# Spectral mixing and GEGLU on one core: modulation rows, half of the soft thresholds, and the order of weight preparation, moved between engines

## The chip, the core and the metric

The kernel runs on one core of a Trainium2 chip. A core has TensorE (PE; its weight loads are listed as PEld), VectorE (DVE), ScalarE (ACT), GpSimd (POOL) and SyncE (SP, which here issues every DMA). Each engine works through its own instructions in order and waits on semaphores for the others. SBUF is the on-chip memory, PSUM the accumulators that TensorE writes, 128 partitions each. The metric is the device time of one execution in microseconds (us).

## The reference

Input `x` is 8192 rows of D = 448. A vector `c` gives six modulation rows of 448 (shift, scale and gate for each of two blocks). The first block is a Fourier filter: layer norm, real FFT along the 8192 rows, a complex two-layer MLP in four blocks of 112 channels with a ReLU between, a soft threshold with 0.01, the inverse FFT. The second is a GEGLU with 1792 hidden channels.

```
mod = (_silu(c) @ w_mod).reshape(c.shape[0], 6, 1, -1)
sa, ca, ga, sb, cb, gb = (mod[:, 0], mod[:, 1], mod[:, 2], mod[:, 3], mod[:, 4], mod[:, 5])
h = _layernorm(x, axis=-1) * (1 + ca) + sa
x = x + ga * _A_ref(h, A_w1, A_b1, A_w2, A_b2)
h = _layernorm(x, axis=-1) * (1 + cb) + sb
x = x + gb * _B_ref(h, B_w_gate, B_w_up, B_w_down)
...
lam = 0.01
mr = jnp.abs(or_) - lam
or_ = jnp.sign(or_) * mr * (mr > 0)
```

The threshold equals `y - min(max(y, -lam), lam)`, and also `min(y + lam, relu(y - lam))`.

## The kernel before

The FFT over 8192 = 128 x 64 is done in two stages of matmuls, and every matmul of the filter is split in a high and a low part to keep fp32 accuracy. There are three phases. **Phase A** (to about 80 us) loads `x`, normalises it and does the 128-point transform, storing the result `td` in HBM. **Phase B** (about 80 to 440 us) does the 64-point transform, the filter's MLP, the threshold and the first inverse transform, and beside it prepares what phase C needs. **Phase C** (about 440 us to the end) does the last inverse transform and the GEGLU over 32 chunks of rows, whose down product is a seven-product Strassen form.

Phase B works on 32 units (half of the channels, four frequency rows: `h, bt`) in a software pipeline of steps, `step(i)`. Step i issues the load `tr` of unit i+2; the 64-point transform of unit i on TensorE (`stage_s2`: 24 short matmuls; ACT writes the high part `zh`, then DVE the low part `zl`); the split `th`/`tl` of unit i+1 (ACT, POOL); the second MLP layer, the threshold and the split `yh`/`yl` of unit i-2 in two halves p = 0, 1 (`stage_m2`: DVE writes the clipped value `t` at line 462 and four pieces of `y` at line 470, ACT copies to `yh`, POOL subtracts to `yl`); the inverse transform of unit i-3 (`stage_i1`, ACT copies `us`, which is stored to HBM); and the first MLP layer of unit i-1 (`stage_m1`: ACT writes `hh` with a ReLU, DVE the low part `hl`). The order within a step is written out by hand (`manual_schedule`), and each engine keeps it. A step is counted below from the start of its `zl` on DVE: step 2 begins at 94.27 us, step 12 at 241.25, step 31 at 415.34.

Preparation is hung into the steps through `at(step, hook, function)`, with the hooks `load`, `pe`, `act`, `dve`, `pool` at fixed places of a step: `load` and `pe` stand first, `act` after the split of unit i+1, `dve` after the second half's `yh`, just ahead of `stage_m1`. Hung in are: the four modulation rows `cb`, `sb`, `ga`, `gb` (load of a 448 x 448 matrix as four slices of 112 partitions; `mod_sum` multiplies slice k by `cs[:, k]` and adds, all on POOL, lines 633 to 636; `mod_row` sums over partitions with a ones matmul `psm`, line 640, and ACT copies the row out), `row_scales` (maxima of two rows, as small operations let out one at a time by `drip()`), the norms of the gate and up weights (`squares` on ACT, `norms` on PE, `norms_out` `nrm` on DVE, steps 1 to 16), the seven Strassen combinations of the down weights (`down_sums`: a reduction on DVE, four POOL subtractions on `m`), from step 18 the scaled gate and up weights (`weights_hi` on ACT, `weights_lo` on DVE for pr = 0 and on POOL for pr = 1), and three scaled down weights (`down_hi` on ACT line 867, `down_lo` on DVE line 871).

## Time and profile before

| | |
|---|---|
| median of 3 runs | 2016.21 us (2015.73 to 2016.96) |
| profiled execution | 2015.64 us, span 2013.8 us, mean granted clock 0.977 |
| busy | PE 1914.2 us (95%), DVE 1136.5 (56%), ACT 764.7 (38%), POOL 1232.5 (61%) |
| DMA | 165.75 MB, mean 82 GB/s |

The span is the time from the first to the last instruction; the profiled execution's own time is 1.84 us longer. A row of the timeline gives the start and the length in us, engine, line, operation, what is written and read, its shape and, in square brackets, how long the engine sat idle before it and what ended that. `x2` or `x4` is the number of instructions merged in a row. In the table by windows come, for each stretch, its length, the busy time and number of instructions of PE, PEld, DVE, ACT and POOL, the granted clock of TensorE (1.00 is full speed), the share of DMA busy and GB/s. "Granted clock" is what the throttle let TensorE have.

### The profile page before, as it was taken

What the parts mean: (1) busy time and instruction counts of PE and PEld (TensorE: products, weight loads), DVE (VectorE), ACT (ScalarE), POOL (GpSimd) and SP (SyncE); (2) the same over time, 40 slices, a digit from 0 to 9 for tenths busy, and PEclk for the clock granted to TensorE, in tenths of its full rate; (3) what the DMA queues carried; (4) which work ended last, traced back from release to release, by engine and by line L of the source; (5) the groups of instructions that cost most, each with busy time, mean ns of one, the idle gap of its engine ahead of it and who ended that gap; (6) DMA issues with size and microseconds to landing.
All of it is one profiled execution on the core that took longest, in us unless ns stands there. A gap on an engine that the chain in (4) does not pass through costs nothing.

```text
span 2013.8 us, 43386 instructions
## 1 busy us (share of the span) xinstructions
PE 1914.2 (95%) x17622; PEld 1700.3 (84%) x17622; DVE 1136.5 (56%) x2351; ACT 764.7 (38%) x1286; POOL 1232.5 (61%) x1532
## 2 busy tenths in 40 slices
PE   7857799979999999999999999999999999999999
PEld 3557789967888989898888888888888888889898
DVE  8536689876655555555455555555555555555533
ACT  5534457745233333333333333333333333333322
POOL 4257656636566666666666666666666666666644
PEclk9878899989999999999999999999999999999999
DMA  9856666742211111111111111111111111111000
GB/s 345 296 153 214 218 205 192 215 118 82 62 44 43 43 42 43 43 43 43 43 43 49 44 45 50 42 42 42 46 47 42 42 42 42 43 42 43 22 17 20
DMA packets 147851, 165.75 MB, mean 82 GB/s; under 512 B 83953, under 2 KB 121585, under 8 KB 147266
## 3 DMA queue, kind: packets, MB, share of 16 engines
q1 hardware_dynamic: 147650, 162.97, 26.6%
q8 instruction: 138, 2.26, 0.5%
q14 instruction: 63, 0.52, 0.1%
HBM read 97.49 MB, written 49.66 MB: 73 GB/s over the span
## 4 chain that ended last, share of the span: by engine, by line
PE 82%; DVE 7%; POOL 4%; DMA 2%; ACT 2%; issue 1%; SPq 0%; DVEq 0%; ACTq 0%; POOLq 0%
PE pgu L1034 50%; PE pdn L1102 7%; PE pdn L1100 7%; PE pdn L1101 7%; DVE y L470 2%; PE ps L212 1%; DMA td<-xt 1%; POOL raw L635 1%; PE pi L934 1%; DVE t L462 1%; DVE zl L385 1%; POOL raw L636 1%; PE pi L932 1%; DVE hl L440 1%; PE pi L933 1%
## 5 line engine op out<-in xcount | busy, mean ns | idle before, releaser
L1034 PE MATMUL pgu<-nt,wh 128*128 128x256 f16 x6272 | 834.3, 273 | 1.6 <-DVE nt L1025 1.6
L1034 PEld LDWEIGHTS <-wh 128*128 128x128 f16 x6272 | 602.7, 98 | 99.3 <-issue 31.7
L1070 ACT ACTIVATE gel<-pgu,dg 128x256 f32<-128x256 f32 x448 | 200.3, 473 | 797.4 <-PE pgu L1034 762.1
L1034 PE MATMUL pgu<-nt,wl 128*128 128x256 f16 (+1 forms) x3584 | 501.3, 272 | 0.0
L1100 PE MATMUL pdn<-wd,ac 128*128 128x224 f16 x1568 | 406.1, 259 | 2.0 <-ACT p L1129 2.0
L1102 PE MATMUL pdn<-wd,ac 128*128 128x224 f16 x1568 | 406.1, 259 | 0.2 <-DVE ac L1093 0.2
L1101 PE MATMUL pdn<-wd,ac 128*128 128x224 f16 x1568 | 406.1, 259 | 0.0
L1081 POOL TENSOR_TENSOR x<-x 128x128 f32<-128x128 f32 x223 | 243.4, 1091 | 235.5 <-DVE x L1075 235.5
L1093 DVE SCALAR_TENSOR_TENSOR ac<-x,sa_act,ac 128x896 f16<-128x896 f32 (+1 forms) x225 | 310.4, 1380 | 84.6 <-ACT ac L1092 84.6
L1034 PEld LDWEIGHTS <-wl 128*128 128x128 f16 (+1 forms) x3584 | 297.9, 97 | 57.2 <-issue 23.9
L1075 DVE TENSOR_TENSOR x<-pgu,gel 128x256 f32<-128x256 f32 x448 | 179.6, 418 | 285.0 <-ACT gel L1070 284.4
L1092 ACT ACTIVATE ac<-x,sa_act 128x896 f16<-128x896 f32 (+1 forms) x225 | 232.9, 1035 | 52.5 <-POOL x L1084 50.5
L1135 POOL TENSOR_TENSOR o<-u,p 128x224 f32<-128x224 f32 x32 | 21.1, 658 | 291.9 <-DVE u L1134 291.9
L1082 POOL TENSOR_TENSOR x<-x 128x128 f32<-128x128 f32 x223 | 159.1, 714 | 17.5
L1101 PEld LDWEIGHTS <-ac 128*128 128x128 f16 x1568 | 153.4, 98 | 2.5 <-issue 2.2
L1100 PEld LDWEIGHTS <-ac 128*128 128x128 f16 x1568 | 153.4, 98 | 0.6 <-issue 0.2
L1102 PEld LDWEIGHTS <-ac 128*128 128x128 f16 x1568 | 153.4, 98 | 0.5 <-DVE ac L1093 0.5
L108 POOL TENSOR_TENSOR yl<-y,yh 128x448 fp32r<-128x448 f32 x63 | 77.7, 1234 | 76.6 <-ACT yh L106 75.4
L1083 POOL TENSOR_TENSOR x<-x 128x128 f32<-128x128 f32 x223 | 114.7, 514 | 0.0
L1084 POOL TENSOR_TENSOR x<-x 128x128 f32<-128x128 f32 x223 | 107.6, 483 | 0.0
L470 DVE TENSOR_TENSOR y<-pm,t 64x224 f32<-64x224 f32 x256 | 99.5, 389 | 8.6 <-DVE t L462 0.5
L108 POOL TENSOR_TENSOR tl<-tr,th 128x896 f16<-128x896 f32 x30 | 57.3, 1910 | 71.3 <-ACT th L106 59.3
(291 smaller groups left out, 2824.7 us busy)
## 6 DMA issues: line engine op xcount, KB each, us to landing
tr<-td SPq DMA_DIRECT2D x64, 224.0 KB, 4.6
raw<-in_gu SPq DMA_DIRECT2D x28, 512.0 KB, 6.3
vd<-us SPq DMA_DIRECT2D x64, 224.0 KB, 3.0
xx<-in_x SPq DMA_DIRECT2D x32, 448.0 KB, 3.3
v<-vd SPq DMA_DIRECT2D x64, 224.0 KB, 2.8
out<-x SPq DMA_DIRECT2D x31, 448.0 KB, 2.7
nt<-pk SPq DMA_TRANSPOSE x480, 2.3
tb<-in_x SPq DMA_DIRECT2D x8, 896.0 KB, 17.5
```

The lines of the kernel that those rows point to most:

```text
L108: (el or V).tensor_tensor(lo, src, h, ALU.subtract)
L470: V.tensor_tensor(y[ri * 64 : ri * 64 + 64, gi], pv[si, ri], tv[si, ri], ALU.subtract)
L1034: T.matmul(pgu[i, t, q][:, pr * H : (pr + 1) * H], w[rows, tw, f0 : f0 + 128], nts[i][rows, tn, :], start=start, stop=stop, skip_group_che ...
L1070: S.activation(gl, ps[:, :H], AF.Gelu_apprx_tanh, scale=dg)
L1075: V.tensor_tensor(dst, ps[:, H : 2 * H].rearrange("p (b c) -> p b c", b=2), gl.rearrange("p (b c) -> p b c", b=2), ALU.mult)
L1081: e.tensor_tensor(s1, a21, a22, ALU.add)
L1082: e.tensor_tensor(s2, s1, a11, ALU.subtract)
L1092: S.activation(ac[:, 0, k], x[:, k], AF.Copy, scale=sc)
L1093: V.scalar_tensor_tensor(ac[:, 1, k], x[:, k], sc, ac[:, 0, k], op0=ALU.mult, op1=ALU.subtract)
L1100: T.matmul(ps, ac[:, 0, ka], wds[t][:, 0, kb], start=t == 0, stop=False)
L1101: T.matmul(ps, ac[:, 0, ka], wds[t][:, 1, kb], start=False, stop=False)
L1102: T.matmul(ps, ac[:, 1, ka], wds[t][:, 0, kb], start=False, stop=t == NP - 1)
```

## The change

Four things change, all in phase B.

1. **Modulation rows.** The matrix is loaded whole into one tile `wm` (one buffer) in place of two DMAs into the shared `raw` buffers. `mod_sum` multiplies the four slices on ACT (`Copy` with a per-partition scale) and adds two pairs in one POOL instruction of 896 columns; the last addition, `mod_sum2`, comes one step later in the `act` hook; and the ones matmul follows one step after that. Loads move from the `load` hook of steps 1, 3, 5, 8 to the `dve` hook of steps 1, 4, 7, 10; the products to steps 2, 5, 8, 11, `mod_sum2` to 3, 6, 9, 12 and the ones matmul to 4, 7, 10, 13 (from 3, 5, 7, 10).
2. **Soft threshold.** The half p = 1 of each unit is formed as `min(y + lam, relu(y - lam))`: the ReLU by ACT, with the bias in a tile `neglam`, in place of DVE's clip, and the four pieces of `y` by a `scalar_tensor_tensor` on DVE in place of a subtraction.
3. **Down combinations** are loaded in steps 2, 3, 5, 6, 9, 11, 12 (from 4, 6, 7, 9, 11, 12, 14) and formed a step later; `row_scales` moves from step 6 to 7.
4. **Scaled down weights** are made in steps 23, 25, 27 (from 23, 26, 29).

```diff
+    neglam = cpool.tile([128, 1], F32, name="neglam")
+    V.memset(neglam, -LAM)
...
-            V.tensor_scalar(t, ps[:, :D], LAM, -LAM, op0=ALU.min, op1=ALU.max)
+            if p:
+                S.activation(t, ps[:, :D], AF.Relu, bias=neglam)
+            else:
+                V.tensor_scalar(t, ps[:, :D], LAM, -LAM, op0=ALU.min, op1=ALU.max)
...
-                    V.tensor_tensor(y[ri * 64 : ri * 64 + 64, gi], pv[si, ri], tv[si, ri], ALU.subtract)
+                    o = y[ri * 64 : ri * 64 + 64, gi]
+                    if p:
+                        V.scalar_tensor_tensor(o, pv[si, ri], LAM, tv[si, ri], op0=ALU.add, op1=ALU.min)
+                    else:
+                        V.tensor_tensor(o, pv[si, ri], tv[si, ri], ALU.subtract)
...
-            return pool.tile([128, 4, 256], F32, tag="raw", name="raw", bufs=6 if pool is npool else 4)
+            return pool.tile([128, 4, 256], F32, tag="raw", name="raw", bufs=4)
...
-            out = []
-            for i in range(2):
-                wm = raw_tile(pool).rearrange("p q c -> p (q c)")[:112, : 2 * D].rearrange("p (q c) -> p q c", q=2)
-                dma(wm, wmod[q][:, 2 * i : 2 * i + 2])
-                out += [wm[:, 0], wm[:, 1]]
-            return out
+            wm = pool.tile([112, 4, D], F32, tag="wm", name="wm", bufs=1)
+            dma(wm, wmod[q])
+            return wm
 
         def mod_sum(key):
             r = raws[key]
-            G.tensor_scalar(r[0], r[0], cs[:, 0:1], None, op0=ALU.mult)
-            for k in range(1, 4):
-                G.tensor_scalar(r[k], r[k], cs[:, k : k + 1], None, op0=ALU.mult)
-                G.tensor_tensor(r[0], r[0], r[k], ALU.add)
+            for k in range(4):
+                S.activation(r[:, k], r[:, k], AF.Copy, scale=cs[:, k : k + 1])
+            G.tensor_tensor(r[:, 0:2], r[:, 0:2], r[:, 2:4], ALU.add)
+
+        def mod_sum2(key):
+            r = raws[key]
+            G.tensor_tensor(r[:, 0], r[:, 0], r[:, 1], ALU.add)
...
-        for n, (key, q, dst) in zip((1, 3, 5, 8), (("cb", 4, cb_r), ("sb", 3, sb_r), ("ga", 2, ga_r), ("gb", 5, gb_r))):
-            at(n, "load", pre, npool, key, load_mod_row, q)
+        for n, (key, q, dst) in zip((1, 4, 7, 10), (("cb", 4, cb_r), ("sb", 3, sb_r), ("ga", 2, ga_r), ("gb", 5, gb_r))):
+            at(n, "dve", pre, npool, key, load_mod_row, q)
             at(n + 1, "dve", mod_sum, key)
-            at(n + 2, "pe", mod_row, key, dst)
+            at(n + 2, "act", mod_sum2, key)
+            at(n + 3, "pe", mod_row, key, dst)
...
-        for t, n in enumerate((4, 6, 7, 9, 11, 12, 14)):
+        for t, n in enumerate((2, 3, 5, 6, 9, 11, 12)):
...
-        at(6, "dve", row_scales)
+        at(7, "dve", row_scales)
...
-            at(22 + 3 * t, "load", load_d, fp, t, 1)
-            at(23 + 3 * t, "act", down_hi, t)
-            at(23 + 3 * t, "dve", down_lo, t)
+            at(22 + 2 * t, "load", load_d, fp, t, 1)
+            at(23 + 2 * t, "act", down_hi, t)
+            at(23 + 2 * t, "dve", down_lo, t)
```

Three places where the order of an engine moves. First POOL, from step 6 on, before: the second half's `yl`, the seven operations of a modulation row, and the first two of `row_scales` (line 515 is the helper that lets them out).

```order
L108 TENSOR_TENSOR yl<-y,yh 128x448 x2
L633 TENSOR_SCALAR raw<-raw,cs 112x448
L635 TENSOR_SCALAR raw<-raw,cs 112x448
L636 TENSOR_TENSOR raw<-raw 112x448
L635 TENSOR_SCALAR raw<-raw,cs 112x448
L636 TENSOR_TENSOR raw<-raw 112x448
L635 TENSOR_SCALAR raw<-raw,cs 112x448
L636 TENSOR_TENSOR raw<-raw 112x448
L515 TENSOR_SCALAR cb_r<-cb_r 128x448
L515 TENSOR_SCALAR hb<-rmax 128x1
L108 TENSOR_TENSOR tl<-tr,th 128x896
```

In the change the row's work on POOL is two additions in two steps, with the next unit's `tl` between them (here the second row, steps 5 to 7):

```order
L641 TENSOR_TENSOR wm<-wm 112x896
L110 TENSOR_TENSOR tl<-tr,th 128x896
L645 TENSOR_TENSOR wm<-wm 112x448
L110 TENSOR_TENSOR yl<-y,yh 128x448 x2
L795 TENSOR_TENSOR m<-m 128x224
L796 TENSOR_TENSOR m<-m 128x224
L797 TENSOR_TENSOR m<-m 128x224
L798 TENSOR_TENSOR m<-m 128x224
L110 TENSOR_TENSOR tl<-tr,th 128x896
L110 TENSOR_TENSOR yl<-y,yh 128x448 x2
```

The pair addition (line 641) follows step 5's `yl`, and the last addition (line 645) stands before step 6's; the seven operations in a row are gone. The next five rows are again four down combinations, those of step 7, and then `cb_r`, the first of `row_scales`. Then ACT in step 5 (in the change the step of a modulation row's products), from the first half's `yh` to `zh` of the next step:

```order
L108 CAST yh<-y 128x448
L465 ACTIVATE t<-pm_1442,neglam 128x448
L511 COPY us<-pi_1463 128x448
L511 COPY us<-pi_1468 128x448
L108 CAST yh<-y 128x448
L640 ACTIVATE wm<-wm,cs 112x448 x4
L441 ACTIVATE hh_759<-pm_1484 112x2x256
L441 ACTIVATE hh_760<-pm_1500 112x2x256
L386 ACTIVATE zh_755<-ps_1536,ca_101 112x2x256
```

The `t` of the second half (line 465) stands behind the first half's `yh`, and the four products (line 640) stand ahead of both `hh`; before, `yh`, `us`, `us`, `yh`, `hh`, `hh` followed each other. Last DVE in step 7, where the rows' maxima are taken (`t`, `y` of the first half, `y` of the second, `hl`):

```order
L467 TENSOR_SCALAR t<-pm_1731 128x448
L479 TENSOR_TENSOR y<-pm_1731,t 64x224 x4
L477 SCALAR_TENSOR_TENSOR y<-pm_1755,t 64x224 x4
L791 TENSOR_REDUCE dn<-m 128x1
L442 SCALAR_TENSOR_TENSOR hl<-pm_1800,hh_759 112x2x256
L442 SCALAR_TENSOR_TENSOR hl<-pm_1817,hh_760 112x2x256
L524 TENSOR_REDUCE rmax<-cb_r 128x1
L688 TENSOR_SCALAR nrm<-pw 128x2
L387 SCALAR_TENSOR_TENSOR zl<-ps_1853,ca_101,zh_755 112x2x256
```

The second half's `t` is gone from DVE, and `rmax`, which reads POOL's `cb_r`, stands ahead of the next step's `zl`, as it did before in step 6.

## The prediction

> **What bounds the kernel now.** I read the table by windows first, to find the stretch that the change can touch, then the groups of waits there, then the timeline of DVE.

> ```profile
> 130.00:230.00 100.00, 67.16 (x574) 61.56 (x573) 54.15 (x121) 41.42 (x73) 68.76 (x91) 0.81 0.57 188
> 230.00:350.00 120.00, 116.39 (x1097) 111.98 (x1095) 104.12 (x219) 82.09 (x134) 73.61 (x72) 0.99 0.71 216
> PE psm L640 <- POOL raw L636: 43.5, 4, 11.4
> ```

> None of phase C's code changes, so I look at phase B alone. In 130 to 230 us TensorE is busy two thirds of the time; the wait behind it is the last row: four times, 43.5 us in all, the ones matmul `psm` waits for POOL's seven operations. TensorE's queue stands behind it, so everything stands. What that costs is read from the starts of `zl`, one or two per step:

> ```profile
> 94.27 1.42 DVE L385 SCALAR_TENSOR_TENSOR zl<-ps,ca,zh 112x512 fp32r<-112x512 f32 x2
> 126.03 1.42 DVE L385 SCALAR_TENSOR_TENSOR zl<-ps,ca,zh 112x512 fp32r<-112x512 f32 x2 [0.31 <-ACT zh L384]
> 157.39 1.42 DVE L385 SCALAR_TENSOR_TENSOR zl<-ps,ca,zh 112x512 fp32r<-112x512 f32 x2 [0.25 <-ACT zh L384]
> 188.45 0.75 DVE L385 SCALAR_TENSOR_TENSOR zl<-ps,ca,zh 112x512 fp32r<-112x512 f32 x1 [0.26 <-ACT zh L384]
> 198.03 0.75 DVE L385 SCALAR_TENSOR_TENSOR zl<-ps,ca,zh 112x512 fp32r<-112x512 f32 x1
> 231.21 1.43 DVE L385 SCALAR_TENSOR_TENSOR zl<-ps,ca,zh 112x512 fp32r<-112x512 f32 x2 [0.31 <-ACT zh L384]
> 241.25 1.42 DVE L385 SCALAR_TENSOR_TENSOR zl<-ps,ca,zh 112x512 fp32r<-112x512 f32 x2 [0.42 <-ACT zh L384]
> 250.06 1.42 DVE L385 SCALAR_TENSOR_TENSOR zl<-ps,ca,zh 112x512 fp32r<-112x512 f32 x2 [0.26 <-ACT zh L384]
> 267.63 1.40 DVE L385 SCALAR_TENSOR_TENSOR zl<-ps,ca,zh 112x512 fp32r<-112x512 f32 x2
> ```

> Two undisturbed steps take 267.63 - 250.06 = 17.57 us, 8.8 each. There `zl` still waits 0.2 to 0.3 us for TensorE's transform (by ACT's `zh`), so TensorE sets the pace, and DVE alone would need about 8.5.

> **A, the POOL chain goes.** The pairs of steps with a row take 31.76, 31.36 and 31.06 us, against 17.6: 14.2, 13.8 and 13.5 too much. The fourth lies in the steps of the units with frequency 0, whose undisturbed pitch is 9.6 (188.45 to 198.03) and 10.0 (231.21 to 241.25): 33.18 - 19.6 = 13.6. Sum **-55.1**. It exceeds the 43.5 since TensorE restarts at half clock.

> **B, the row's new work.** The products stand on ACT just ahead of `hh`, for which DVE's `hl` waits, and for that TensorE's next `stage_m2`.

> ```profile
> 306.70 1.27 ACT L384 ACTIVATE zh<-ps,ca 112x512 fp32r<-112x512 f32 x2
> L384 ACT ACTIVATE zh<-ps,ca 112x512 fp32r<-112x512 f32 x48 | 32.0, 693 | 11.9 <-PE ps L378 11.4 <-ACT zh L384 0.3
> L439 ACT ACTIVATE hh<-pm 112x512 fp32r<-112x512 f32 x44 | 23.9, 592 | 2.2 <-PE pm L427 2.2
> L502 ACT COPY us<-pi 128x448 f32<-128x448 f32 x46 | 22.2, 532 | 1.6 <-PE pi L501 1.6
> 111.17 1.86 PE psm L640 x2
> 108.00:112.00 4.00, 0.83 (x1) 0.50 (x2) 0.00 (x0) 0.00 (x0) 3.03 (x3) 0.50 0.27 78
> ```

> `zh` has a per-partition scale as the products have: two in 1.27 us, one 0.69, so a pitch of 0.58 for 512 columns, about 0.53 for 448. Four: 2.1 us per row, **+8.4** (between 0, if ACT were early enough, and 4 x 4 x 0.69 = 11). The ones matmul takes 1.86 us; the last row shows the half clock (0.50) it ran at, so I take half, 0.93, on the pacing engine: **+3.7** (to 7.4). POOL's two additions have slack.

> A gap has a second price:

> ```profile
> 288.00:292.00 4.00, 2.27 (x17) 1.75 (x15) 3.79 (x10) 1.33 (x3) 3.05 (x5) 1.00 0.70 192
> 292.00:296.00 4.00, 3.94 (x18) 3.79 (x19) 1.24 (x4) 1.03 (x4) 1.94 (x2) 0.57 0.20 42
> 348.00:352.00 4.00, 3.18 (x40) 2.99 (x39) 3.94 (x5) 3.94 (x8) 3.67 (x3) 1.00 0.59 161
> 376.00:380.00 4.00, 1.25 (x12) 1.06 (x11) 3.97 (x4) 3.97 (x6) 2.62 (x2) 1.00 0.83 194
> 380.00:384.00 4.00, 4.00 (x22) 3.83 (x21) 3.72 (x9) 0.83 (x3) 0.16 (x2) 0.60 0.45 154
> ```

> After 1.73 and 2.75 us of TensorE idle in a slice the next 4 us run at 0.57 and 0.60 of the clock, which loses 4 x 0.43 = 1.7 us; after 0.82 us nothing happens. Products make a gap of about 2.1 + 0.2 us, so each row costs a cold stretch in the step behind it: **+6.7**.

> [...]

> **C, the threshold.** The clip's group, and an undisturbed step on DVE and ACT:

> ```profile
> L462 DVE TENSOR_SCALAR t<-pm 128x448 f32<-128x448 f32 x47 | 29.1, 620 | 1.6 <-PE pm L454 0.9
> 243.31 1.59 DVE L470 TENSOR_TENSOR y<-pm,t 64x224 f32<-64x224 f32 x4
> 245.66 1.60 DVE L470 TENSOR_TENSOR y<-pm,t 64x224 f32<-64x224 f32 x4
> 244.99 0.57 ACT L106 CAST yh<-y 128x448 fp32r<-128x448 f32 x1 [1.32 <-DVE y L470]
> 245.46 0.96 ACT L502 COPY us<-pi 128x448 f32<-128x448 f32 x2
> ```

> Before, the second half's `y` follows the first's after 0.76 us (244.90 to 245.66, with DVE's own `t`). After, ACT first makes `yh` (starts 0.09 later, next instruction 0.47 on), then the ReLU: `us`'s 0.53 plus 0.10 for the pointer operand (693 against 592), then 0.03 to DVE: 1.22. DVE is freed of 0.62 us but waits longer: +0.46 per step. The new form of `y` is not in the trace; I price it as the old one of the same shape, and 0.03 apiece more would be +4. In steps 2, 5, 8, 11, 14, 15 TensorE's lead takes 0.25 of it: 6 x 0.21 = 1.3; in the steps behind products or with a ones matmul TensorE is later anyway: 0. From step 16 DVE sets the pace: 16 x 0.46 = 7.4, and 3 x 0.46 = 1.4 in the drain. **+10.1** (0, if `yh` and ReLU were to hide, to 15).

> [...]

> **D, `row_scales` in step 7.** In step 12, built like step 7:

> ```profile
> 249.65 0.15 DVE L679 TENSOR_SCALAR nrm<-pw 128x2 f32<-128x2 f32 x1
> 251.84 1.90 POOL L108 TENSOR_TENSOR tl<-tr,th 128x896 f16<-128x896 f32 x1
> 174.52 1.34 POOL L515 TENSOR_SCALAR cb_r<-cb_r 128x448 f32<-128x448 f32 x1
> ```

> DVE is free for `rmax` at 249.65; POOL ends its four combinations at 251.84 and would then need 1.34 for `cb_r`: 253.2, a stall of 3.5 us. In step 6 of before it lay inside A, and so did the two `rmax` and smaller operations, which stay: by the width of `t` (0.62) some 1.4 us. **+4.9** (1.4 to 6.5).

> **E, down weights.**

> ```profile
> 342.18 1.40 DVE L385 SCALAR_TENSOR_TENSOR zl<-ps,ca,zh 112x512 fp32r<-112x512 f32 x2
> 346.79 0.55 ACT L106 CAST yh<-y 128x448 fp32r<-128x448 f32 x1
> 351.46 1.40 DVE L385 SCALAR_TENSOR_TENSOR zl<-ps,ca,zh 112x512 fp32r<-112x512 f32 x2
> 368.37 1.40 DVE L385 SCALAR_TENSOR_TENSOR zl<-ps,ca,zh 112x512 fp32r<-112x512 f32 x2
> 379.56 1.40 DVE L385 SCALAR_TENSOR_TENSOR zl<-ps,ca,zh 112x512 fp32r<-112x512 f32 x2
> 388.95 1.42 DVE L385 SCALAR_TENSOR_TENSOR zl<-ps,ca,zh 112x512 fp32r<-112x512 f32 x2
> ```

> Step 23 (pr = 1) takes 9.28, step 26 (DVE has `weights_lo` and `down_lo` behind each other) 11.19 and leaves a cold 27 of 9.39; plain steps (351.46 to 368.37 is two) 8.46. All three now stand in pr = 1, so 26 saves 1.9 and 27 about 0.9. But there ACT reaches `yh` only at 346.79, after both weights, and the ReLU is late with it: `y` at 346.79 + 0.45 + 0.66 = 347.9 against 346.57, 0.87 more than C's 0.46, three times 2.6. Net about 0. These steps then leave TensorE some 2.4 us idle and the next one cold, about 0.9 each: **+2.6**.

> **Sum:** -55.1 + 8.4 + 3.7 + 6.7 + 10.1 + 4.9 + 2.6 = -18.7. On the profiled execution's 2015.64 (span 2013.8) that is 1996.9; its median is 0.57 higher, so **1997**.

> **Rivals.**

> *The clock stays up* (27%). Gaps of 2.3 us may straddle whatever is looked at; only two cases speak for cold stretches. Without 6.7 and 2.6, but with C's 0.21 in four more steps: 1989. [...]

> *Everything new is hidden* (8%): products and ones matmul cost nothing either. Another 12 us: 1977. `hl`'s wait for `hh` speaks against it, which already is the tail of each step.

> *The matrix comes too late* (14%), the case that ends on the other side.

> ```profile
> raw<-in_mod SPq DMA_DIRECT2D x8, 392.0 KB, 7.2
> wdd<-m SPq DMA_DIRECT2D x7, 784.0 KB, 6.2
> 131.23 1.12 SPq L504 DMA_DIRECT2D vd<-us x2
> ```

> `wm` (784 KB, one buffer) is issued behind `vd`, 6.3 us into its step, and needed some 6.7 us into the next: 9.4 us. Median landings are 6.2 to 7.2 us, but POOL no longer spaces the other transfers: steps 1 to 12 move the same bytes in less time. Each us of lateness stops ACT ahead of `hh` and so all engines, four times. From 9.4 + 4.7 = 14 us of landing time nothing is left and it is slower, over 2016; 2 to 3 us late gives about 2007. 3% for the whole.

> The rest, 5%, is for a ReLU that costs over 1 us a step where ACT is full.

> **The numbers.** My own sum has 46%, with 1991 to 2004. 1981 to 2009 leaves out most of the hidden case and the late tail. About 4 us (0.2%) is what this kernel's timing can tell from no change: faster 0.92, same 0.05, slower 0.03.

> **What would show it.** The wait of `psm` for POOL is gone; steps with products are about 11.1 us from `zl` to `zl`, with DVE's `hl` waiting some 3.3 us for `hh`, and a granted clock near 0.6 in the slice behind; plain steps from 18 on about 8.9 to 9.0 instead of 8.5, with DVE idle some 1.2 us ahead of the second `y`, put down to ACT; `rmax` waiting 3.5 us for POOL; phase C the same to 1 us. I am wrong if the first product waits for a DMA by more than 1 us, if plain steps stay at 8.5, or if no slice outside the old ones is cold.

## The result, and the profile after

The changed kernel takes **1992.86 us** (median of 4 runs, 1990.49 to 1994.25), against 2016.07 (4 runs, 2015.73 to 2016.96): 0.9883 of the time, with a 95% interval of 0.9866 to 0.99. The profiled execution took 1993.32 us with a span of 1991.4, 22.4 less than the span before. The prediction was 1997, with 1981 to 2009.

The timeline of DVE in the changed kernel, where `zl` opens each step (steps 2 to 8, 14, 16 and 31), and the last `yl` of phase B:

```profile
93.83 1.42 DVE L387 SCALAR_TENSOR_TENSOR zl<-ps,ca,zh 112x512 fp32r<-112x512 f32 x2 [0.27 <-ACT zh L386]
104.83 1.40 DVE L387 SCALAR_TENSOR_TENSOR zl<-ps,ca,zh 112x512 fp32r<-112x512 f32 x2
116.77 1.42 DVE L387 SCALAR_TENSOR_TENSOR zl<-ps,ca,zh 112x512 fp32r<-112x512 f32 x2 [1.32 <-ACT zh L386]
125.78 1.40 DVE L387 SCALAR_TENSOR_TENSOR zl<-ps,ca,zh 112x512 fp32r<-112x512 f32 x2
137.00 1.40 DVE L387 SCALAR_TENSOR_TENSOR zl<-ps,ca,zh 112x512 fp32r<-112x512 f32 x2
147.66 1.42 DVE L387 SCALAR_TENSOR_TENSOR zl<-ps,ca,zh 112x512 fp32r<-112x512 f32 x2 [1.33 <-ACT zh L386]
160.91 0.74 DVE L387 SCALAR_TENSOR_TENSOR zl<-ps,ca,zh 112x512 fp32r<-112x512 f32 x1
...
228.36 1.40 DVE L387 SCALAR_TENSOR_TENSOR zl<-ps,ca,zh 112x512 fp32r<-112x512 f32 x2
...
246.32 0.74 DVE L387 SCALAR_TENSOR_TENSOR zl<-ps,ca,zh 112x512 fp32r<-112x512 f32 x1
...
393.52 1.40 DVE L387 SCALAR_TENSOR_TENSOR zl<-ps,ca,zh 112x512 fp32r<-112x512 f32 x2
...
416.35 0.63 DVE L110 TENSOR_TENSOR yl<-y,yh 128x448 fp32r<-128x448 f32 x1 [0.69 <-ACT yh L108]
```

The same places in the kernel before, for the stretches that the prediction did not show (steps 14, 16, 31 and the last `yl`):

```profile
258.81 1.43 DVE L385 SCALAR_TENSOR_TENSOR zl<-ps,ca,zh 112x512 fp32r<-112x512 f32 x2 [0.20 <-ACT zh L384]
...
276.33 0.75 DVE L385 SCALAR_TENSOR_TENSOR zl<-ps,ca,zh 112x512 fp32r<-112x512 f32 x1 [0.17 <-ACT zh L384]
...
415.34 1.40 DVE L385 SCALAR_TENSOR_TENSOR zl<-ps,ca,zh 112x512 fp32r<-112x512 f32 x2
436.57 0.63 DVE L108 TENSOR_TENSOR yl<-y,yh 128x448 fp32r<-128x448 f32 x1 [0.69 <-ACT yh L106]
```

Cut at these starts, the 22.4 us lie here. The forecast column is the prediction's terms, put into the stretches that they belong to:

| stretch | before | after | difference | forecast |
|---|---|---|---|---|
| up to step 2 | 94.27 | 93.83 | -0.4 | 0 |
| steps 2 to 13 (A, B, D, a little of C) | 164.54 | 134.53 | -30.0 | -30.6 |
| steps 14, 15 (C) | 17.52 | 17.96 | +0.4 | +0.4 |
| steps 16 to 30 (C, E) | 139.01 | 147.20 | +8.2 | +9.5 |
| step 31 and drain (C) | 21.23 | 22.83 | +1.6 | +1.9 |
| phase C | 1577.2 | 1575.05 | -2.2 | 0 |

Step 2 with a row's products takes 104.83 - 93.83 = 11.00 us and step 5 11.22; the two others lie in the frequency-0 steps (12.61 and 12.71). The plain steps 14 and 15 take (246.32 - 228.36) / 2 = 8.98. What the engines wait for between 85 and 300 us (us in total, times, longest):

```profile
DVE hl L442 <- ACT hh L441: 25.5, 16, 3.4
DVE y L477 <- ACT t L465: 22.9, 19, 1.3
...
PE pm L451 <- ACT hh L441: 7.2, 5, 2.3
...
POOL wm L641 <- ACT wm L640: 4.4, 4, 1.1
DVE rmax L524 <- POOL cb_r L524: 3.6, 1, 3.6
```

TensorE's four waits for POOL with 43.5 us are gone. Each new wait is the size of a term: the products hold `hh` and so `hl` up; the second half's `y` waits for the ReLU; `rmax` waits once for POOL. The new form of `y` costs no more than the old one:

```profile
L477 DVE SCALAR_TENSOR_TENSOR y<-pm,t 64x224 f32<-64x224 f32 x128 | 49.8, 389 | 44.3 <-ACT t L465 43.0
L479 DVE TENSOR_TENSOR y<-pm,t 64x224 f32<-64x224 f32 x128 | 49.8, 389 | 4.1
```

### The profile page after: what moved, and what is told of

Read it like the earlier page. It is cut to its first block, busy times and chain, and to the rows that moved or that the text cites. A ratio compares the mean times of both kernels' runs of the same rounds, so it can differ in the third digit from the quotient of the medians.

```text
span 1991.4 us, 43353 instructions
## 1 busy us (share of the span) xinstructions
PE 1923.5 (97%) x17622; PEld 1709.7 (86%) x17622; DVE 1112.1 (56%) x2320; ACT 789.9 (40%) x1334; POOL 1209.0 (61%) x1512
## 4 chain that ended last, share of the span: by engine, by line
PE 81%; DVE 8%; ACT 4%; POOL 3%; issue 2%; DMA 1%; SPq 1%; ACTq 0%; DVEq 0%; POOLq 0%
PE pgu L1044 50%; PE pdn L1110 7%; PE pdn L1112 7%; PE pdn L1111 7%; PE ps L214 3%; DVE y L477 2%; DVE y L479 1%; DVE hl L442 1%; PE pi L944 1%; ACT t L465 1%; PE pi L942 1%; DMA tr<-td 1%; PE pi L943 1%; DVE zl L387 1%; ACT yh L108 1%
## 5 line engine op out<-in xcount | busy, mean ns | idle before, releaser
L1044 PEld LDWEIGHTS <-wl 128*128 128x128 f16 (+1 forms) x3584 | 297.8, 97 | 57.2 <-issue 23.9
L1092 POOL TENSOR_TENSOR x<-x 128x128 f32<-128x128 f32 x223 | 160.1, 718 | 17.5
L1124 POOL TENSOR_TENSOR o<-o,gb_r 128x448 f32<-128x448 f32 (+1 forms) x64 | 71.7, 1120 | 8.1 <-DVE o L1134 5.6
```

Source lines behind the costliest of these rows:

```text
L1044: T.matmul(pgu[i, t, q][:, pr * H : (pr + 1) * H], w[rows, tw, f0 : f0 + 128], nts[i][rows, tn, :], start=start, stop=stop, skip_group_che ...
L1092: e.tensor_tensor(s2, s1, a11, ALU.subtract)
```

## The experiments

Each ratio below is to the kernel before on the same chip. My theory going in was the prediction's own list of terms; the rival for each was that the term is hidden, or priced in the wrong place.

### The change without the threshold

```
-            if p:
-                S.activation(t, ps[:, :D], AF.Relu, bias=neglam)
-            else:
-                V.tensor_scalar(t, ps[:, :D], LAM, -LAM, op0=ALU.min, op1=ALU.max)
+            V.tensor_scalar(t, ps[:, :D], LAM, -LAM, op0=ALU.min, op1=ALU.max)
...
-                    o = y[ri * 64 : ri * 64 + 64, gi]
-                    if p:
-                        V.scalar_tensor_tensor(o, pv[si, ri], LAM, tv[si, ri], op0=ALU.add, op1=ALU.min)
-                    else:
-                        V.tensor_tensor(o, pv[si, ri], tv[si, ri], ALU.subtract)
+                    V.tensor_tensor(y[ri * 64 : ri * 64 + 64, gi], pv[si, ri], tv[si, ri], ALU.subtract)
```

> The change without its threshold part: both halves are clipped by DVE again, all else as changed. Theory (ACT's ReLU stands behind the first half's yh, so each step waits for the crossing, and in the three down-weight steps for both weights too): plain steps from 18 on go back from 9.06 to 8.5 us, the three down-weight steps from some 10.8 to 9.3 and the cold steps behind them (9.4) to 8.5, the drain is 1.6 shorter; together some 15 us, so about 1978. Rival (the ReLU costs nothing net, the steps are long for another reason, such as more ACT work or later transfers): 1990 to 1994, plain steps still 9.0.

Measured: 1970.47 us (1969.73 to 1971.2), 0.977 of before (0.9755 to 0.9784). The threshold costs 22.4 us within the change, more than any theory allowed (the largest expected some 15). By the starts of `zl`, 7.7 of it lie in steps 3 to 12, 2.6 in 16 and 17, 2.5 in the five plain steps 18 to 22 (0.50 each, as predicted), 8.3 in steps 23 to 30 (with the down weights) and 1.6 in the drain. So half of it isn't the plain crossing (DVE's wait for the ReLU on ACT, 0.50 us a plain step): it comes where ACT has other new work. This opened the question that most of the later runs are for.

### The ReLU ahead of the first half's yh on ACT

```
-                y = stage_m2(*units[i - 2], 0)
-                ys = [split_y(y)]
+                y0 = stage_m2(*units[i - 2], 0)
                 y = stage_m2(*units[i - 2], 1)
+                ys = [split_y(y0)]
```

(and the same in `m2_i1` for the drain.)

> The change with one order swapped: in every step the second half's ReLU is issued ahead of the first half's yh on ACT, so that it runs while DVE still forms the first half's y. Same instructions. Theory (the price is the place in ACT's queue, not the operation): DVE no longer waits for t and is rid of the clip's 0.73 us, plain steps from 18 on fall below the old 8.5 to TensorE's 8.2 or so, about 1972. Rival (the price is the ReLU's time on ACT or the new form of y): plain steps stay at 8.8 to 9.1, 1985 to 1993.

Measured: 1965.91 us (1964.28 to 1967.31), 0.9747 (0.9732 to 0.9761): 27 us faster than the change, and 4.6 faster than without the threshold. The plain steps 21, 22, 29 and 30 take 8.15 to 8.23, as the theory had it; its time, about 1972, was 6 us too long. ACT and DVE in a plain step of the changed kernel (the y of the second half is L477):

```profile
388.16 0.57 ACT L108 CAST yh<-y 128x448 fp32r<-128x448 f32 x1 [1.44 <-DVE y L479]
388.63 0.63 ACT L465 ACTIVATE t<-pm,neglam 128x448 f32<-128x448 f32 x1
...
389.37 1.60 DVE L477 SCALAR_TENSOR_TENSOR y<-pm,t 64x224 f32<-64x224 f32 x4 [1.30 <-ACT t L465]
```

and in this run:

```profile
272.50 0.64 ACT L465 ACTIVATE t<-pm,neglam 128x448 f32<-128x448 f32 x1 [0.51 <-PE pm L456]
...
273.46 1.60 DVE L477 SCALAR_TENSOR_TENSOR y<-pm,t 64x224 f32<-64x224 f32 x4
```

In the change ACT idles 1.44 us for the first half's `y` and only then makes the ReLU, whose input TensorE had finished 1.9 us earlier (386.70 us); one place earlier in ACT's queue it is done before DVE asks, and `y` follows without a wait. It was the order of two instructions on ACT, not the ReLU's length (0.63 and 0.64), that cost.

### The products split two and two into ACT's idle places

```
+            at(n + 2, "act", mod_mul, key, (0, 1))
+            at(n + 2, "mid", mod_mul, key, (2, 3))
+            at(n + 2, "dve", mod_sum, key)
+            at(n + 3, "act", mod_sum2, key)
+            at(n + 4, "pe", mod_row, key, dst)
...
-        at(7, "dve", row_scales)
+        at(9, "dve", row_scales)
```

("mid" is a new place between `stage_i1` and the second `split_y`; `mod_mul` makes the products that `mod_sum` made. The rows are loaded in steps 1, 5, 9 and 13 instead of 1, 4, 7 and 10, and their products stand in steps 3, 7, 11 and 14.)

> The change with the modulation rows' four products taken from ahead of hh and put, two and two, into ACT's two idle spots of a step (ahead of the first half's yh and behind us), rows loaded in steps 1, 5, 9, 13, row_scales in step 9, where no down combinations stand ahead of it. Theory (products delay hl by 2.25 us, the gap they make leaves TensorE cold in the step behind, row_scales waits 3.6 us for the combinations): products' steps fall from 11.0 to about 9.1, no cold slice behind them, and only the ones matmul's 0.9 is left in the step that it ends; some 9 + 4 + 2.7 less, about 1977. Rival 1 (no cold cost; the long step behind is the ones matmul): that step stays at 10.7, about 1981. Rival 2 (transfers set the pace of steps 1 to 14): about 1990.

Measured: 1976.49 us (1976.31 to 1977.26), 0.98 (0.9786 to 0.9815), as expected. The start of step 16 comes 14.7 us earlier than in the change. Steps 6 and 7, which took 10.66 and 13.25, take 8.98 and 9.06 in this run, like plain ones, although step 7 now holds the second row's products (step 6 holds none, and `row_scales` has left step 7):

```profile
131.85 1.40 DVE L387 SCALAR_TENSOR_TENSOR zl<-ps,ca,zh 112x512 fp32r<-112x512 f32 x2
140.83 1.40 DVE L387 SCALAR_TENSOR_TENSOR zl<-ps,ca,zh 112x512 fp32r<-112x512 f32 x2
149.89 0.74 DVE L387 SCALAR_TENSOR_TENSOR zl<-ps,ca,zh 112x512 fp32r<-112x512 f32 x1
```

Steps 3 and 14, which hold products as well, take 9.00 and 9.06. So the multiplications themselves need not cost anything; what cost was that they stood together ahead of `hh`. How much of the 16.4 us gained on the change is due to the moved `row_scales` this run alone does not say.

### The down weights back in steps 23, 26 and 29

```
-            at(22 + 2 * t, "load", load_d, fp, t, 1)
-            at(23 + 2 * t, "act", down_hi, t)
-            at(23 + 2 * t, "dve", down_lo, t)
+            at(22 + 3 * t, "load", load_d, fp, t, 1)
+            at(23 + 3 * t, "act", down_hi, t)
+            at(23 + 3 * t, "dve", down_lo, t)
```

> The change with the scaled down weights back in steps 23, 26, 29. Theory (moving them saves step 26's pile-up on DVE and costs a third late ReLU and cold step, net about 0): 1992 to 1995. Rival (the move is a gain of its own): 1996 to 1998; (the move is a loss): 1988 to 1990.

Measured: 1993.59 us (1991.81 to 1996.75), 0.9885 (0.9869 to 0.9902): the same within the scatter. Steps 23 to 30 take 78.75 us here and 78.68 in the change.

### The threshold alone, on the kernel before

```
-            V.tensor_scalar(t, ps[:, :D], LAM, -LAM, op0=ALU.min, op1=ALU.max)
+            if p:
+                S.activation(t, ps[:, :D], AF.Relu, bias=neglam)
+            else:
+                V.tensor_scalar(t, ps[:, :D], LAM, -LAM, op0=ALU.min, op1=ALU.max)
```

(with the change's new form of `y` for the second half.)

> The kernel before with the threshold of the change alone: ReLU on ACT for the second half of each step, the old multiplications on POOL, the old places of the down weights. If the threshold's cost is the crossing alone (+0.46 us a step where DVE sets the pace, 0 in the steps that POOL's chain holds up): +9 to +12 against before, about 2027, as the prediction's term C has it. If the 22 us that leaving it out of the change gained are its own cost everywhere: +20 or more, 2036 and up. A result near 2027 would say that the other 10 us come from its meeting with the rows' products and with the down weights in TensorE's gaps.

Measured: 2028.0 us (2026.97 to 2028.54), 1.0058 (1.0041 to 1.0075): +11.4 us. Its waits from 85 to 430 us hold both kinds:

```profile
PE psm L649 <- POOL raw L645: 45.3, 4, 11.9
DVE y L477 <- ACT t L465: 36.8, 28, 2.2
```

The expected 9 to 12 us (about 2027) is met; 20 and more (2036 and up) is not. So the crossing by itself is what the prediction said, and the 11 us more within the change come from its meeting with other parts of the change.

### The change with the products hidden and without the threshold

The edit joins those of "the change without the threshold" and "the products split two and two".

> The run with the products in ACT's idle places (1976.5), and without the ReLU: DVE clips both halves as before. With the change (1992.9), the change without threshold (1970.5) and the products hidden (1976.5) this completes a square. The threshold alone cost 11.4 us on the kernel before and 22.4 us within the change. Theory (10 us of these 22 come from its meeting with other work on ACT: the rows' products in steps 2 to 12, and the down weights, behind which the ReLU queues in steps 23, 25 and 27): hiding the products takes away only the first part of the meeting, so the threshold costs 15 to 19 us here, 1958 to 1961. If the meeting is with the products alone: 11 to 12 us, 1964 to 1965. If the products have nothing to do with it: 22 us, 1954.

Measured: 1958.29 us (1957.88 to 1958.68), 0.9709 (0.9692 to 0.9727). The threshold costs 1976.5 - 1958.3 = 18.2 us here, in the theory's range. This completes a square:

| | rows as changed | rows hidden | kernel before |
|---|---|---|---|
| no ReLU | 1970.5 | 1958.3 | 2016.6 |
| ReLU as changed | 1992.9 | 1976.5 | 2028.0 |
| ReLU first | 1965.9 | 1955.9 | not run |

By the starts of `zl`, the threshold costs 7.7 us in steps 3 to 12 with the rows as changed and 3.1 with them hidden: 4.6 is the meeting with the products (on the kernel before it costs 3.7 there). In steps 23 to 30 it costs 8.3 in the change, 8.7 with the rows hidden and 5.3 on the kernel before: there it meets the moved down weights. Without the ReLU the move makes these steps 2.8 us shorter (70.37 against 73.16 before); with it they take the same in the old places and in the new. The trace of the changed kernel shows the meeting: in a step with down weights (25) the second `y` waits 2.54 us for a ReLU that stands behind three weight operations on ACT, in the next one 1.30:

```profile
340.99 1.59 DVE L477 SCALAR_TENSOR_TENSOR y<-pm,t 64x224 f32<-64x224 f32 x4 [2.54 <-ACT t L465]
...
350.78 1.60 DVE L477 SCALAR_TENSOR_TENSOR y<-pm,t 64x224 f32<-64x224 f32 x4 [1.30 <-ACT t L465]
```

### TensorE's gap behind the products filled

```
+        def filler():
+            ps = bank("pd", "dum")
+            for k in range(24):
+                T.matmul(ps[:, :128], ident, ident, start=True, stop=True)
...
             at(n + 2, "act", mod_sum2, key)
+            at(n + 2, "act", filler)
```

> The change, with 24 matmuls of 128 columns (identity by identity, nobody reads them) put into TensorE's queue in steps 3, 6, 9 and 12 between the second transform and the first stage_m2, which is where TensorE stands idle for hh behind the products (2.30, 1.52, 1.48 and 1.17 us in the changed kernel). By the pitch of the transform's matmuls (0.056 us) they take 1.3 us and leave gaps of at most 1.0 us; they do no useful work. Theory (a gap of over about 1 us makes the clock fall for the next 3 to 4 us, and that is the 1.7 us a row of the prediction): the granted clock stays at 1.00 behind them and the run is 4 to 7 us shorter than the changed kernel's 1992.9, about 1987. Rival (the clock falls for another reason, or cold matmuls hide behind DVE): no gain, 1992 to 1996.

Measured: 1992.05 us (1986.71 to 1993.14), 0.9875 (0.986 to 0.9891). By its time the run is inconclusive: the gain of 0.8 us is inside the scatter. Its profile isn't. The filler takes 1.50 us in step 3 and leaves a gap of 0.96 instead of 2.30:

```profile
103.78 1.50 PE L646 MATMUL dum<-ident 128*128 128x128 f16 x24
106.24 0.37 PE L451 MATMUL pm<-w2h,hh 113*128 113x224 f32 x1 [0.96 <-ACT hh L441]
```

The granted clock is 1.00 in the stretches behind the three gaps (107.44 to 110.86, 138.16 to 141.58 and 209.85 to 213.26 us), and steps 3, 6 and 12 take 9.10, 9.21 and 9.21 us instead of 11.94, 10.66 and 10.72: 5.8 us less. Steps 3 and 6 are sure: in four profiles without a filler (the change, its second profile below, and the runs on the down weights and on `row_scales`) they take 10.67 to 12.10 and 10.66 to 12.26. Step 12 is not: it takes 9.21 without a filler too, in one of the four. Steps 9 and 10 give 1.6 back (12.86 and 11.10 instead of 12.22 and 10.17), with half clock from 182.54 to 185.95 us, where the change has a granted clock of 1.00. And this profiled execution began step 2 2.7 us later (96.50 us instead of 93.83), since ACT's first `th` waited longer for its load. The change's row first, then this run's:

```profile
78.61 0.94 ACT L108 CAST th<-tr 128x896 f16<-128x896 f32 x1 [3.15 <-DMA tr<-td]
```

```profile
80.75 0.94 ACT L108 CAST th<-tr 128x896 f16<-128x896 f32 x1 [7.10 <-DMA tr<-td]
```

The filler is not in that load's way; in the 12 other profiles of the study step 2 begins at 93.5 to 95.1. So the cold stretch behind the products (0.50 in the change, 1.00 here) is real, about 1.9 us in each of these three steps on average, but what else differs from profile to profile is as large.

### row_scales ahead of POOL's combinations

```
             at(n + 1, "dve", down_sums, t)
+            at(n + 1, "pool" if n == 6 else "dve", down_combos, t)
```

(`down_sums` keeps its reduction; its four subtractions became `down_combos`.)

> The change, with POOL's four combinations of the down matrix in step 7 queued behind stage_m1 instead of ahead of it; everything else, the reduction on DVE too, stays. Theory (term D: rmax waits for cb_r only because POOL has those four ahead): the wait of rmax falls from 3.6 to under 1.5 us, TensorE's gap of 2.9 us behind it falls by as much, and the time falls by 3 to 5 us, to about 1989. Rival (TensorE or ACT would have held the step up anyway): under 1 us of gain.

Measured: 1991.53 us (1985.13 to 1993.97), 0.9873 (0.9854 to 0.9892): not to be told from the change, so the expected gain of 3 to 5 us does not show in the time. The wait did fall, from 3.62 (first row, changed kernel) to 0.86 us (second fence, this run), and step 7 from 13.25 to 10.49:

```profile
160.30 0.62 DVE L524 TENSOR_REDUCE rmax<-cb_r 128x1 f32<-128x448 f32 x1 [3.62 <-POOL cb_r L524]
```

```profile
158.16 0.62 DVE L524 TENSOR_REDUCE rmax<-cb_r 128x1 f32<-128x448 f32 x1 [0.86 <-POOL cb_r L524]
```

But step 6, in which nothing differs, took 12.24 instead of 10.66. In the stretch that holds TensorE's gap there it was busy for 1.67 of 3.41 us, against 1.75 in the change; it stayed at half clock for 6.83 us after that (135.48 to 142.31) instead of 3.41. What decides that is the next run's question.

### The changed kernel once more

> The changed kernel once more, unaltered, for a second profile. Its runs lie between 1990.5 and 1994.3. In the first profile the stretches at half clock begin at 103.6, 137.7, 168.4, 209.4, 264.1, 325.5, 345.9 and 366.4 us, all whole multiples of 3.413 us apart, and each lasts 3.41 us or a multiple of it; a stretch follows where TensorE was busy for less than 0.59 of the 3.413 us before, and does not where it was busy for over 0.60. Theory (the clock is set for such stretches from a grid that runs freely, so it is chance how a gap falls into it): the same grid at another offset, the same bound, and another set of cold stretches, with some steps 1 to 2 us longer or shorter than in the first profile. Rival (the gap's own length decides, wherever it falls): the same steps are cold for as long, and the pitches agree to 0.2 us.

Measured: 1993.77 us (one run). The grid of the expectation is there: up to step 30, cold stretches (those at half clock) begin at 105.78, 136.50, 170.63, 262.79 and 344.71 us, 9, 19, 46 and 70 times 3.413 us behind the first, and each lasts 3.41, 6.83 or 10.24 us. The set of them differs, as the theory said. First profile, stretches cut at the grid (columns: length, busy time of PE, PEld, DVE, ACT and POOL with instructions, granted clock, DMA share, GB/s):

```profile
100.19:103.61 3.42, 1.12 (x21) 0.98 (x18) 0.06 (x2) 3.38 (x7) 1.62 (x2) 1.00 1.06 300
103.61:107.02 3.41, 3.41 (x15) 3.18 (x15) 2.82 (x6) 3.33 (x5) 2.56 (x2) 0.50 1.06 369
107.02:110.43 3.41, 3.41 (x15) 3.28 (x15) 2.02 (x6) 1.10 (x2) 2.64 (x3) 0.50 0.27 105
...
134.33:137.74 3.41, 1.75 (x13) 1.57 (x14) 2.02 (x5) 3.41 (x7) 2.11 (x1) 1.00 1.02 406
137.74:141.15 3.41, 3.41 (x17) 3.32 (x16) 2.74 (x6) 1.81 (x3) 2.92 (x2) 0.50 1.10 314
141.15:144.57 3.42, 3.42 (x27) 3.35 (x27) 2.57 (x5) 2.48 (x6) 1.55 (x3) 1.00 0.84 298
...
206.01:209.42 3.41, 2.00 (x18) 1.67 (x15) 2.08 (x5) 3.41 (x7) 2.10 (x1) 1.00 1.07 329
209.42:212.84 3.42, 3.42 (x19) 3.42 (x18) 2.68 (x6) 1.81 (x4) 2.99 (x2) 0.50 1.05 363
```

Second profile of the same kernel:

```profile
133.09:136.50 3.41, 1.65 (x23) 1.32 (x20) 0.83 (x2) 3.41 (x7) 2.30 (x2) 1.00 1.01 408
136.50:139.92 3.42, 3.42 (x17) 3.42 (x17) 2.78 (x6) 2.56 (x4) 2.58 (x2) 0.50 1.13 310
139.92:143.33 3.41, 3.41 (x13) 3.19 (x13) 2.04 (x7) 1.63 (x3) 2.40 (x3) 0.50 0.92 365
143.33:146.74 3.41, 3.41 (x27) 3.20 (x27) 2.53 (x4) 1.95 (x4) 1.84 (x3) 1.00 0.47 122
...
208.18:211.60 3.42, 2.25 (x18) 2.07 (x18) 2.52 (x5) 3.42 (x7) 2.12 (x2) 1.00 1.14 314
211.60:215.01 3.41, 3.41 (x30) 3.35 (x29) 2.24 (x6) 1.81 (x3) 3.30 (x3) 1.00 0.96 374
```

TensorE's gaps in steps 6 and 12 are equal in both profiles (1.52 us in step 6, 1.17 and 1.16 in step 12):

```profile
135.74 0.37 PE L451 MATMUL pm<-w2h,hh 113*128 113x224 f32 x1 [1.52 <-ACT hh L441]
...
207.36 0.37 PE L451 MATMUL pm<-w2h,hh 113*128 113x224 f32 x1 [1.17 <-ACT hh L441]
```

```profile
135.69 0.37 PE L451 MATMUL pm<-w2h,hh 113*128 113x224 f32 x1 [1.52 <-ACT hh L441]
...
209.10 0.37 PE L451 MATMUL pm<-w2h,hh 113*128 113x224 f32 x1 [1.16 <-ACT hh L441]
```

Yet step 6 takes 10.66 us in the first and 12.26 in the second, step 12 10.72 in the first and 9.21 in the second, where the gap fell into a stretch in which TensorE was busy for 2.25 of 3.41 us (2.00 in the first). The gap's length alone does not decide: the two of 1.52 us were followed by 3.41 and 6.83 us at half clock, and those of 1.17 and 1.16 us, which lie differently on the grid, by 3.41 us and by none. One detail of the expectation was too sharp: one stretch of the second profile with a busy share of 0.58 was followed by full clock.

### Both remedies, and the down-weight steps clipped on DVE

The first kernel joins the edits of "the ReLU ahead" and "the products split"; nothing else is changed.

> The change with both remedies: the products two and two into ACT's idle places with rows at steps 1, 5, 9 and 13 and row_scales in step 9, and the second half's ReLU ahead of the first half's yh on ACT. Alone they gave 1976.5 (-16) and 1965.9 (-27). From the starts of zl: up to step 16 the first saves 14.7 us, and from step 16 to 31 the second saves 14.3 us. If they work on different stretches: 1956 to 1963. If they spend the same slack twice: no better than 1966.

Measured: 1955.86 us (1955.51 to 1958.24), 0.9704 (0.9689 to 0.9718). The two work on different stretches, as expected. In the steps with down weights its second `y` still waits 2.07 us for the ReLU, so one more kernel clips on DVE there alone:

```
-        def stage_m2(h, bt, p):
+        def stage_m2(h, bt, q):
+            p, r = q and (h, bt) not in [units[23 + 2 * t - 2] for t in range(ND)], q
```

(`r` then stands where `p` meant the half, `p` where it means the ReLU.)

> The best run so far (1955.9: products hidden, ReLU first), with DVE's clip instead of the ReLU in steps 23, 25 and 27 only, where ACT has two weight tiles ahead and DVE's y waits 2.07 us for the ReLU. From the starts of zl: a pair of steps with down weights takes 10.45 + 7.84 = 18.3 us there, with the clip on DVE 9.28 + 8.54 = 17.8 in the run without threshold. Theory: 17.3 to 17.8 a pair, 1.5 to 3 us less, 1953 to 1954.5. Rival (DVE's extra 0.62 us takes back what the wait cost): 1955.5 to 1957.

Measured: **1952.68 us** (1951.34 to 1954.99), 0.9683 (0.9668 to 0.9698). It is the fastest kernel here, 40 us below the change and 64 below the kernel before on its chip (2017.1). A pair of steps with down weights takes 9.67 + 7.83 = 17.5 us, as expected. The gain of 3.2 us on the run before it is just over the expected 1.5 to 3.

## Why the prediction was right, and where it was not

The time lies 4 us below the forecast and inside the likeliest case's own range; the mechanism of every large term was seen. Point by point:

- **A, -55.1.** The chain is gone, and steps 2 to 13 together moved by -30.0 where the terms summed to -30.6. No run measures A by itself. The nearest is the one with the products hidden and without the threshold: its steps 2 to 15 are 49.1 us shorter than before (132.98 against 182.06), where A, the ones matmuls and the 1.4 of D make -50.0.
- **B, products and ones matmul, 8.4 + 3.7.** Steps 2 and 5 take 11.00 and 11.22, forecast 11.1, and `hl` waits 3.23 to 3.42 us for `hh`, forecast 3.3. The ones matmul takes 0.91 to 0.92 us, forecast 0.93. So the rival "everything new is hidden" fell. TensorE's gap behind the first row's products, forecast 2.3:

```profile
103.57 0.55 PE L451 MATMUL pm<-w2h,hh 113*128 113x224 f32 x1 [2.30 <-ACT hh L441]
```

- **B, the cold stretch, 6.7.** Right in kind and near in size: filling the gap took 2.84, 1.45 and 1.51 us out of three steps, 1.9 on average where 1.7 a row was set (by the mean of the four unfilled profiles 2.2, 2.2 and 1.1), but nothing out of the third row's step 9. The rival "the clock stays up" fell: it is 0.50 from 103.61, 137.74 and 209.42 us on, behind the products. But I thought of a gap's length as what decides, and in the two profiles of the change gaps of one length were followed by different times at half clock (1.52 us by 3.41 and 6.83, 1.17 and 1.16 us by 3.41 and 0), so 1.7 is a mean over 0 to 2.8, not a price.
- **C, +10.1.** Alone on the kernel before it is 11.4. Plain steps are 9.04 to 9.08, forecast 8.9 to 9.0, and DVE waits 1.30 us, forecast 1.2. Within the change it is 22.4. Of that the working had 10.1 here and 2.6, for the ReLU behind the down weights, under E. One step of it failed: "in the steps behind products or with a ones matmul TensorE is later anyway: 0". Without the ReLU the gap in step 6 shrinks from 1.52 us to 0.82 and TensorE is busy for 2.35 of the 3.41 us around it instead of 1.75, the granted clock is 1.00 from 109.49 to 164.10 and from 167.52 to 252.85 us, and steps 6 and 12 take 9.12 and 9.16 instead of 10.66 and 10.72. The ReLU's lateness and the products' lateness add up on the way to `hh`: behind both together the clock fell to 0.50 in these two steps, behind the products alone it stayed at 1.00. That the sum came out all the same is in part luck: I had put the cold stretches down to the products alone, under B, and the runs show that most of them need the ReLU as well. Without it only two of the four rows, in steps 3 and 8, still have one, of 3.41 us each (from 106.08 and 164.10 us). The 5% for a ReLU over 1 us a step where ACT is full came true in three steps: 23, 25 and 27 take 1.26, 1.64 and 1.63 longer with it.
- **D, +4.9.** The wait is 3.62 us, forecast 3.5; step 7 takes 13.25, and 10.49 with the wait at 0.86 (one profile each), so the stall is worth 2.8.
- **E, +2.6.** Near: in the prediction's terms it is 1.8. Steps 23 to 30 grew by 5.5 us (73.16 to 78.68), of which C has 8 x 0.46 = 3.7. That saving and late ReLU cancel was right (78.68 us in the new places, 78.75 in the old), and each side is near: without the ReLU the move gains 2.8, forecast 1.9 + 0.9, and with it steps 23, 25 and 27 lose 3.1 beyond C's 0.46 each, forecast 2.6. The cold steps behind the down weights (24, 26 and 28, with half clock from 325.48, 345.95 and 366.44 us), set at 0.9 each, take 9.42 to 9.46 against 9.08, 0.4 each. With the ReLU the old places have steps as long (9.45 and 9.41 in steps 24 and 27), and without it there are none (8.54, at a granted clock of 1.00), so they come from the threshold and not from the move. They move as well: the second profile has 9.08 in steps 24 and 28, but 11.01 in step 26, with half clock from 344.71 to 351.54 us. Steps 16 and 17, which I forecast 0.9 longer, are 0.4 longer; they differ by up to 4.3 from kernel to kernel. Steps 16 to 30 together are 1.3 below the forecast.
- **Phase C, "the same to 1 us".** Wrong: 2.2 less, the larger part of the 3.6 us between the sum and the profiled execution. In the 12 other profiles of the study phase C takes 1574.9 to 1576.4 us, the upper end on the kernel before with the threshold alone; the 1577.2 of the profile before is the odd one. I take it for scatter of single executions; no second profile of the kernel before was made.
- **The matrix too late.** It fell: in the change ACT's first product never waits for a DMA, and POOL waits 1.1 us at most for the products themselves.

## What to carry to other kernels

When an operation moves to another engine, look first at where it lands in that engine's queue: here the same ReLU cost 22 us behind an instruction that waits, and gained 5 one place ahead of it. Two latenesses on the way to the same instruction can't be priced one by one, since each uses up the slack of the other, and together they can bring what neither brings alone: here, in steps 6 and 12, two of the rows' four, TensorE's clock fell to 0.50 with both and stayed at 1.00 without the ReLU, and with the products hidden as well. And before two variants are compared to 2 us by one profile each, look at a second profile of the same kernel: its cold stretches move (step 12 took 10.72 us in one and 9.21 in the other).
